# Attention scores as row-tiled quads of heads, with gelu in large blocks: one core, 2048 tokens, 32 heads of 20

## Chip, cores, metric

One core of one Trainium2 chip. The metric is device time in microseconds (us). Most executions of a kernel agree within 0.3%; some are slower. Engines: PE (TensorE), PEld (its weight loads), ACT (ScalarE), DVE (VectorE), POOL (GpSimd), SP (SyncE). "Clock" is the share of full PE clock that was granted. Three ways of placing a matmul on PE occur: column-tiled (`tile_position=(0, 32 * c)`, 32 columns each, four side by side), row-tiled (`tile_position=(32 * i, 0)`, 32 rows each) and untiled (all of PE). Going from one to another is called a change of tiling mode.

## The reference, cut

```python
qkv = xn @ wqkv                          # xn = layernorm(x), 2048 x 640, bf16
p   = softmax(q @ k.T * 20**-0.5)        # 32 heads, head size 20, 2048 x 2048 scores each
s   = (p @ v) @ wo
h   = gelu(layernorm(xn) @ w1)           # four groups of columns, shifted by 1, -1, 2, -2 tokens
x1  = xn + shifted(h) @ w2
g   = silu(x1 + gelu(layernorm(x1) @ w3) @ w4)     # w3: 640 x 1536
out = x + s * g
```

The large term is the softmax: 32 x 2048 x 2048 exponentials, on 128 lanes 1024 instructions of 1024 elements each.

## The kernel before

A planner in the kernel takes tasks with an engine, an estimated duration and the data that they read and write, and fixes each engine's order before launch. Engines then run their lists strictly in that order. MLP matmuls have the lowest priority on PE: they go where the planner believes PE to be idle.

```python
# per query block, per quad of heads: queries of head i masked over 128 rows (6 heads share a stack of rows)
T("pool", c_pool(512), lambda e, ...: e.tensor_scalar(QTP[:, qb, i, :], QT[:, st, q0:q0 + 512],
      self.maskh[:, j:j + 1], 0.0, op0=ALU.mult, op1=ALU.add), ...)
# scores of one head: four 32-column tiles, side by side
for c in range(4):
    ins = e.matmul(pb[32*c:32*c+32, 0:512], KT[:, st, kt*128 + 32*c : kt*128 + 32*c + 32],
                   QTP[:, qb, i, :], start=True, stop=True, tile_position=(0, 32 * c))
# one exp over two heads' scores, in two banks; two such pairs of banks alternate
T("act", c_act(1024), lambda e, ...: e.activation(PT[:, slot, :], self.psum[:, 1024*sb:1024*sb+1024], AF.Exp, ...))
# P*V of four heads: four 22-column tiles;  every other matmul of the kernel is column-tiled too
# gelu: evacuate, x*x, a*x+b, *x on DVE; tanh of 512 elements on ACT; (th+1)*x on DVE: 68 times
```

## Time and profile before

| | before |
|---|---|
| runs | 1073.52 and 1543.01 us, median 1308.26 |
| span of the profiled run | 1071.9 us, mean clock 0.994 |
| first exp / last exp ends / end | 47.1 / 1061.0 / 1071.9 us |
| exps, waits before them | 1024, 17.7 us |

The exps alone fill some 950 us of ACT. The lines are in the prediction below.

### The profile page before, as it was taken

The page shows a single profiled execution, that of the slowest core. Times are in us where ns is not written, and L with a number is a line of the kernel's source. Part 1 is how long each engine was busy: PE and PEld are TensorE (multiplying, and loading weights), DVE is VectorE, ACT ScalarE, POOL GpSimd, SP SyncE. Part 2 cuts the span into 40 slices and gives each one's busy share as a digit, 9 for nine tenths or more (in the row PEclk, how much of TensorE's full clock was granted, in tenths as well). Part 3 has the DMA queues.
Part 4 walks back from the last instruction along what each step waited for, and adds up shares of the span by engine and source line. Part 5 has one row for each costly group of instructions (what it writes and reads, how often), then busy time and mean ns, then how long its engine had stood idle before and what let it go on. Part 6 is the DMA issues. An engine that isn't in the chain of part 4 may idle for free.

```text
span 1071.9 us, 38329 instructions
## 1 busy us (share of the span) xinstructions
PE 937.1 (87%) x17672; PEld 395.9 (37%) x17672; DVE 547.6 (51%) x1272; ACT 1024.4 (96%) x1175; POOL 126.2 (12%) x198
## 2 busy tenths in 40 slices
PE   3899999998978899998999899889999987777786
PEld 2454454432423344443454244224443441111132
DVE  8767766792236577378647557433457310000024
ACT  7588999999989999999999999999999999999995
POOL 4202111121001110111110111110111100011100
PEclk9999999999999999999999999999999999999998
DMA  6000000020001010031111101110011000000000
GB/s 178 16 7 14 14 3 14 7 57 2 3 14 26 22 26 21 2 100 46 27 39 46 32 21 51 33 26 15 15 27 46 27 2 2 1 2 2 1 8 32
DMA packets 62968, 27.52 MB, mean 26 GB/s; under 512 B 53208, under 2 KB 62808, under 8 KB 62808
## 3 DMA queue, kind: packets, MB, share of 16 engines
q1 hardware_dynamic: 62808, 25.08, 9.1%
q8 instruction: 138, 2.26, 0.9%
q14 instruction: 22, 0.18, 0.1%
HBM read 22.45 MB, written 2.62 MB: 23 GB/s over the span
## 4 chain that ended last, share of the span: by engine, by line
ACT 63%; PE 25%; DVE 10%; issue 1%; DMA 0%; SPq 0%; DVEq 0%
ACT arena L1190 59%; PE psum L1184 11%; PE psum L1042 4%; ACT arena L1307 3%; PE psum L1198 3%; PE psum L1407 2%; PE psum L977 1%; DVE arena L1390 1%; PE psum L1470 1%; PE psum L1364 1%; DVE arena L1131 1%; ACT arena L1483 1%; DVE arena L1092 1%; PE psum L1081 1%; DVE arena L1075 1%; DVE arena L802 1%
## 5 line engine op out<-in xcount | busy, mean ns | idle before, releaser
L1190 ACT ACTIVATE arena<-psum 128x1024 bf16<-128x1024 f32 x1024 | 961.4, 1058 | 17.7 <-PE psum L1184 15.8
L1184 PE MATMUL psum<-arena 128*32 128x512 bf16 x8192 | 626.7, 382 | 83.0 <-ACT arena L1190 66.1
L1184 PEld LDWEIGHTS psum<-arena 128*32 128x32 bf16 x8192 | 157.9, 95 | 376.4 <-ACT arena L1190 327.1
L1198 PE MATMUL psum<-arena 128*22 128x512 bf16 x2048 | 199.1, 379 | 0.9 <-ACT arena L1190 0.9
L1167 POOL TENSOR_SCALAR arena<-arena 128x512 bf16<-128x512 bf16 x128 | 95.9, 763 | 677.4 <-PE psum L1184 674.2
L1206 DVE STREAM_TRANSPOSE arena<-psum 128x512 f32<-128x512 f32 x32 | 22.8, 712 | 193.9 <-PE psum L1198 193.8
L1301 DVE CAST arena<-psum 128x512 bf16<-128x512 f32 x68 | 46.8, 688 | 85.8 <-PE psum L1450 47.3
L1450 PE MATMUL psum<-arena 128*32 128x512 bf16 x960 | 79.7, 380 | 7.6 <-DVE arena L1459 7.4
L1042 PE MATMUL psum<-arena 128*32 128x512 bf16 x960 | 74.8, 385 | 2.2 <-ACT arena L895 1.0
L1470 PE MATMUL psum<-arena 128*32 128x320 bf16 x1536 | 74.6, 299 | 1.5 <-DVE arena L1459 1.5
L1198 PEld LDWEIGHTS psum<-arena 128*22 128x22 bf16 x2048 | 52.6, 93 | 57.7 <-ACT arena L1190 1.7
L1470 PEld LDWEIGHTS psum<-arena 128*32 128x32 bf16 x1536 | 40.7, 97 | 32.9 <-DVE arena L1459 3.0
L1459 DVE SCALAR_TENSOR_TENSOR arena<-arena 128x512 bf16<-128x512 bf16 x48 | 33.1, 689 | 28.2 <-ACT arena L1307 27.9
L881 PE MATMUL psum<-arena 128*32 128x128 bf16 x960 | 28.5, 242 | 19.6 <-DVE arena L823 17.8
L1307 ACT ACTIVATE arena<-arena 128x512 bf16<-128x512 bf16 x68 | 45.1, 664 | 0.0
L1236 PE MATMUL psum<-arena 128*32 128x320 bf16 x896 | 44.6, 299 | 0.1
L1364 PE MATMUL psum<-arena 128*32 128x512 bf16 x400 | 34.4, 388 | 9.6 <-DVE arena L1390 8.8
L1450 PEld LDWEIGHTS psum<-arena 128*32 128x32 bf16 x960 | 25.4, 97 | 41.7 <-DVE arena L1459 18.4
L1480 DVE SCALAR_TENSOR_TENSOR arena<-psum,arena 128x320 bf16<-128x320 f32 x32 | 14.7, 486 | 48.2 <-PE psum L1470 45.7
L1246 DVE CAST arena<-psum 128x320 bf16<-128x320 f32 x32 | 14.7, 487 | 44.7 <-PE psum L1236 44.5
L1042 PEld LDWEIGHTS psum<-arena 128*32 128x32 bf16 x960 | 24.9, 98 | 30.0 <-DVE arena L1131 1.9
L881 PEld LDWEIGHTS psum<-arena 128*32 128x32 bf16 x960 | 20.5, 107 | 36.0 <-DVE arena L823 18.8
(104 smaller groups left out, 718.2 us busy)
## 6 DMA issues: line engine op xcount, KB each, us to landing
arena<-in_B_w_dram SPq DMA_DIRECT2D x68, 160.0 KB, 2.5
arena<-in_A_x_dram SPq DMA_DIRECT2D x8, 320.0 KB, 5.9
arena<-in_A_x_dram SPq DMA_DIRECT2D x16, 160.0 KB, 2.2
out_dram<-arena SPq DMA_DIRECT2D x16, 160.0 KB, 1.8
arena<-in_B_w_dram SPq DMA_DIRECT2D x1, 1920.0 KB, 9.3
arena<-in_A_wqkv_dram SPq DMA_DIRECT2D x10, 150.0 KB, 2.8
arena<-in_A_wqkv_dram SPq DMA_DIRECT2D x1, 800.0 KB, 9.7
arena<-in_A_wo_dram SPq DMA_DIRECT2D x4, 200.0 KB
```

Source lines behind the costliest of these rows:

```text
L881: ins = e.transpose(pb[32 * c:32 * c + 32, 128 * bi:128 * bi + 128], src_of(n)[:, kc * 128 + 32 * c: kc * 128 + 32 * c + 32], ident[:, :], ...
L1042: ins = e.matmul(pb[32 * c:32 * c + 32, 0:512], Wst[:, qk, kc, 32 * c:32 * c + 32], xnT[:, kc, c0:c1], start=(kc == 0), stop=(kc == KC - 1 ...
L1167: lambda e, qb=qb, i=i, st=st, j=j, q0=q0: e.tensor_scalar(QTP[:, qb, i, :], QT[:, st, q0:q0 + 512], self.maskh[:, j:j + 1], 0.0, op0=ALU. ...
L1184: ins = e.matmul(pb[32 * c:32 * c + 32, 0:512], KT[:, st, kt * 128 + 32 * c: kt * 128 + 32 * c + 32], QTP[:, qb, i, :], start=True, stop=T ...
L1190: lambda e, sb=sb, slot=slot: e.activation(PT[:, slot, :], self.psum[:, 1024 * sb:1024 * sb + 1024], AF.Exp, scale=cfg.scale),
L1198: ins = e.matmul(pb[32 * i:32 * i + 22, 0:512], VA[:, kt, h, 0:22], PT[:, slots[i // 2], 512 * (i % 2):512 * (i % 2) + 512], start=(kt == ...
L1236: ins = e.matmul(pb[32 * c:32 * c + 32, 0:HALF], OT[:, quad, 128 * nl + 32 * c:128 * nl + 32 * c + 32], Wo[:, quad, hh * HALF:(hh + 1) * H ...
L1301: T("dve", c_dve(512, "psum"), lambda e, h=h: e.tensor_copy(xb, self.wbank(h)[:, 0:512]), reads=[wa], writes=[an(0)], name=f"{tag}_x", rel=h)
L1307: T("act", c_act(512), lambda e: e.activation(thb, wb, AF.Tanh, scale=math.sqrt(2.0 / math.pi)), reads=[an(1)], writes=[an(2)], name=f"{ta ...
L1364: ins = e.matmul(pb[32 * c:32 * c + 32, 0:512], W1s[:, ws, kc, 32 * c:32 * c + 32], y2T[i][:, kc, :], start=(kc == 0), stop=(kc == KC - 1) ...
L1450: ins = e.matmul(pb[32 * c:32 * c + 32, 0:512], W3s[:, ws, kc, 32 * c:32 * c + 32], y3T[i][:, kc, :], start=(kc == 0), stop=(kc == KC - 1) ...
L1470: ins = e.matmul(pb[32 * c:32 * c + 32, 0:HALF], GTb[:, fc, 128 * nl + 32 * c:128 * nl + 32 * c + 32], W4[:, fc, hh * HALF:(hh + 1) * HALF ...
```

## The change

Intent: take work off PE and POOL (row-tiled scores of four heads need neither masked queries nor zero rows), replace the guard against overflow by a bound for each query, walk quad by quad so that a head's projections are made one quad ahead, and run gelu as six large ACT blocks instead of 68 small tanh with DVE work around them. Core of the diff, cuts marked:

```diff
-                                for c in range(4):
-                                    ins = e.matmul(pb[32 * c:32 * c + 32, 0:512], KT[:, st, kt * 128 + 32 * c: kt * 128 + 32 * c + 32],
-                                                   QTP[:, qb, i, :], start=True, stop=True, tile_position=(0, 32 * c))
+                    return e.matmul(out, KT[32 * i:32 * i + 21, b, 128 * kt:128 * kt + 128], QT[32 * i:32 * i + 21, b, q0:q0 + 512],
+                                    start=True, stop=True, tile_position=(32 * i, 0))
 ...
+                        T("pe", 240, fn, reads=krd + qrd, writes=[("S", 2 * sb), ("S", 2 * sb + 1)], name=f"sc{self.step}")
 ...  (order: for quad: prepare quad + 1; for query block: for key tile.  Before: for query block: for quad)
 ...  (guard: per head max|k| times |q| by one small matmul, stored by DMA in row 20 of each head's 32 rows)
-        T("act", c_act(512), lambda e: e.activation(thb, wb, AF.Tanh, scale=math.sqrt(2.0 / math.pi)), ...)
+                T("act", 2600 + c_act(KC * 1024),
+                  lambda e, c0=c0: e.activation(hx[:, :, c0:c0 + 1024], hx[:, :, c0:c0 + 1024], AF.Gelu_apprx_tanh), ...)
+        T("act", 2600 + c_act(FC * 512), lambda e: e.activation(GT[:, :, :], GT[:, :, :], AF.Gelu_apprx_tanh), ...)
```

The new code can also give key tiles to DVE, but the table that says how many holds zeros only.

## The prediction

> **What bounds the kernel now.** I read the busy shares first, then the costliest groups, then who ScalarE (ACT) waited for, then ACT and TensorE (PE) in order of time.
>
> ```profile
> span 1071.9 us, 38329 instructions
> PE 937.1 (87%) x17672; PEld 395.9 (37%) x17672; DVE 547.6 (51%) x1272; ACT 1024.4 (96%) x1175; POOL 126.2 (12%) x198
> ACT  7588999999989999999999999999999999999995
> PEclk9999999999999999999999999999999999999998
> ACT 63%; PE 25%; DVE 10%; issue 1%; DMA 0%; SPq 0%; DVEq 0%
> L1190 ACT ACTIVATE arena<-psum 128x1024 bf16<-128x1024 f32 x1024 | 961.4, 1058 | 17.7 <-PE psum L1184 15.8
> L1184 PE MATMUL psum<-arena 128*32 128x512 bf16 x8192 | 626.7, 382 | 83.0 <-ACT arena L1190 66.1
> L1198 PE MATMUL psum<-arena 128*22 128x512 bf16 x2048 | 199.1, 379 | 0.9 <-ACT arena L1190 0.9
> L1167 POOL TENSOR_SCALAR arena<-arena 128x512 bf16<-128x512 bf16 x128 | 95.9, 763 | 677.4 <-PE psum L1184 674.2
> L1307 ACT ACTIVATE arena<-arena 128x512 bf16<-128x512 bf16 x68 | 45.1, 664 | 0.0
> ```
>
> ACT bounds the span: 1024 softmax exponentials of 1024 elements per partition. They waited for PE only 17.7 us. The order of time says where:
>
> ```profile
> 46.45 0.60 ACT L1065 ACTIVATE arena<-psum 128x512 bf16<-128x512 f32 x1 [8.88 <-PE psum L1042]
> 47.10 1.02 ACT L1190 ACTIVATE arena<-psum 128x1024 bf16<-128x1024 f32 x1
> 74.95 1.02 ACT L1190 ACTIVATE arena<-psum 128x1024 bf16<-128x1024 f32 x1 [1.13 <-PE psum L1184]
> 959.52 99.69 ACT L1190 ACTIVATE arena<-psum 128x1024 bf16<-128x1024 f32 x108
> 1059.94 1.02 ACT L1190 ACTIVATE arena<-psum 128x1024 bf16<-128x1024 f32 x1 [0.72 <-PE psum L1184]
> ```
>
> So the time has three parts: 47.1 us until the first exp, 1013.9 us of ACT stream (47.1 to 1061.0), 10.9 us of tail. The waits for PE lie mostly between 70 and 92 us, where the next heads' projections crowd PE. The 108 exps give a step of (99.69 - 1.02)/107 = 0.922 us.
>
> PE is next. Its 87% overstates it, since overlapping matmuls are counted to their ends; the spacing of dense groups gives the real cost:
>
> ```profile
> 72.57 1.90 PE L1042 MATMUL psum<-arena 128*32 128x512 bf16 x32
> 48.87 0.45 PE L977 MATMUL psum<-arena 128*32 128x320 bf16 x8
> 901.10 0.61 PE L1184 MATMUL psum<-arena 128*32 128x512 bf16 x8 [0.30 <-ACT arena L1190]
> ```
>
> Four 32-column matmuls run side by side: a group of width 512 costs (1.90 - 0.39)/7 = 0.216 us (0.39 is one group alone), one of 320 costs 0.45 - 0.31 = 0.14, and I estimate 0.06 for 128. By instruction counts, before has 3188 groups of 512, 960 of 320, 240 of 128: 689 + 134 + 14 = 837 us. At full clock that fits under ACT. It does not when the clock falls: PE alone would need 1543 us at a mean clock of about 837/(1543 - 20) = 0.55. I take this as the cause of the second run quoted for before (1543.01 against 1073.52); the trace shows only the fast state (mean clock 0.994).
>
> **What the Trainium skill says.**
> 1. "ScalarE: Activation LUTs", What ACT_TABLE_LOAD costs: one element per cycle whatever the function; a switch of table set is 1283 ns of load, 2.66 us with its drain. The trace has one load, of 1.28 us, so exp and tanh share a set here; no drain is visible in it.
> 2. "TensorE: Matmul & The Clock Gate", Part 3: matmuls in different 32-row groups run concurrently (four of K=32, N=512 ran 3.07 times as fast). The trace has column groups only, which do run together.
> 3. "TensorEngine Tiling (Array Packing)", Key Properties: "Changing tiling mode (not just tile) drains the TensorE". This trace never changes mode.
> 4. The TensorE page again, Part 1: an idle window of about 3.4 us drops the PE clock to half. The trace's gaps are below that.
>
> **The change, part by part.**
>
> *Scores.* Before: each head's queries are masked on POOL (L1167, 128 x 763 ns) and multiplied over 128 rows, so an exp needs two groups, 0.43 us. After: four heads lie at row tiles of 32 and an exp needs two 21-row matmuls of 128 columns in different row groups and banks, 0.216 us if they overlap. Saved: 1024 x 0.216 = 221 us of PE and all 96 us of POOL, both off the path. The exps are unchanged: 1024, none given to VectorE (the table that would do so holds zeros).
>
> *Projections.* Padding to 32 costs PE 320 groups instead of 240 (+17 us); the squared-norm matmuls go (-10 us). PE after: 837 - 221 + 17 - 10 = about 624 us, plus drains. At least two mode changes per exp; a drain exposes about 0.39 - 0.216 = 0.17 us, so 2 x 1024 x 0.17 = 350 us, total about 970. Still under ACT's 1014, but thin in the stages with MLP matmuls.
>
> *VectorE.* The five-instruction gelu chain (688 + 437 + 309 + 456 + about 690 ns, 68 times) becomes one evacuation: -68 x 1.9 = -129 us. Other per-head guard work shrinks too. All hidden before: no gain in time, only fewer late releases.
>
> *ACT stream, before.* In the stretch 640 to 700 us a tanh takes a slot of 0.52 and a silu tanh 0.62 us: 68 x 0.52 + 16 x 0.62 = 45.3. With 1.5 for late query copies and 16.7 of waits, the exps have 1013.9 - 63.5 = 950, 0.927 each.
>
> *ACT stream, after.* Exps 950. Gelu on whole blocks: two of 5120 and four of 6144 elements at 0.833 ns (0.427 us per 512) plus about 0.15: 2 x 4.4 + 4 x 5.3 = 30. Silu: eight of 1280, 8 x 1.16 = 9. Gelu needs another table set: each of six goes there and back, 12 loads. At 1.28 us: 15; at 2.66: 32. I take 1.6: 19. Sum 1008, against 997 before without waits. Thus the batching saves 45 - 39 = 6 us and pays back 15 to 32 in table loads: a net loss of about 12.
>
> *Waits in the stream.* Most of the 16.7 us came from projections crowding PE, now spread over quads and with scores half as dear. I keep 8.
>
> *Start.* The last LayerNorm write on ACT is at 20.2 us before and after. Then transposes, evacuated alternately by ACT and VectorE without the accumulator reads (0.2 us each on 12), done at about 27; last K and Q tiles 2 x 5 x 0.216 + 0.7 = 3, at 30. The new bound is a serial chain: max over 2048 (a 512 max takes 0.68; 2.3), mask 0.2, matmul 0.39, evacuation 0.69, a DMA into the spare row (about 2.2, as small loads land), score 0.39, with waits 7: 37 us. The quad's weights now come as 40-byte rows in eight DMAs; I add 5 for them and for ordering: 42 against 47.1.
>
> *Tail.* Same chain of transpose, reciprocal, scale, transpose, last output matmuls, store: 11.
>
> Sum: 42 + 1008 + 8 + 11 = 1069 us. Against the fast run (1073.5) that is the same; the large PE saving buys almost nothing there, since PE did not bound it.
>
> In the slow state it buys much: 624/0.55 = 1135 us of PE work plus some 45 of start and tail, about 1180 against 1543.
>
> **The rivals.**
> - *PE becomes the bound through mode drains.* For: the skill's sentence; 0.17 us is more than half a score group. If weight loads (0.095 us) are exposed too, a switch costs 0.27 and two exps in an MLP stage need 0.43 + 0.22 + 0.9 + 4 x 0.27 = 2.6 against 1.85 of ACT. Three of eight quads at up to 1.4 times: up to 140 us more, 1200. Against: the scheduler has freedom to cluster the other matmuls, and most stages have few.
> - *Large gelus starve PE.* An ACT block of 5.3 us plus two loads leaves PE without score banks for about 7 us, enough to drop the clock; six times. Restarting at half clock still gives about 0.86 + 0.43 us per two exps, below 1.85, so perhaps 1 us each: 1075.
> - *The stream closes up more than I think.* Table loads at 1.28, no waits, first exp at 37: 37 + 1004 + 2 + 11 = 1054. This is the floor of the fast state; it is 1.8% below 1073.5.
> - *A late input in a fixed order.* Each engine runs a fixed list; one late gelu input stalls all exps behind it. For: the planner does not model drains. It would add 10 to 40 us.
>
> **Range and chances.** Fast to fast I expect 1069, mostly 1050 to 1100: same 0.65, faster 0.17, slower 0.18. But the time on record for before is 1308, the middle of one fast and one slow run; against that even a mixed pair after, (1069 + 1180)/2 = 1125, is faster by 14%. I do not know which comparison decides; I weigh the median at two thirds: faster 0.67, same 0.25, slower 0.08. The range, 1042 to 1150, holds the fast state and a mixed pair.
>
> **What would show it.** ACT busy about 1025 us again, 13 table loads, exps about 0.93 apart; first exp at 37 to 47; PE busy well below 937 with scores near half of 626.7; POOL under 4%. I am wrong if exps wait for PE by more than 30 us (drains), if a gelu waits for VectorE or PE, if a table load takes far from 1.3 us, or if the first exp comes after 50. A slow run of the changed kernel near 1180 would confirm the clock account of 1543; no slow run at all would leave it open.

## The result

| | before | after |
|---|---|---|
| runs, us | 1073.52, 1543.01 | 1199.82, 1210.49 |
| median, us | 1308.26 | 1205.15 |
| mean clock of the profiled run | 0.994 | 0.751 |

Fast to fast the changed kernel is slower: ratio 1.1227, 95% interval 1.1014 to 1.1441. A ratio here is the mean span of one kernel's fast runs over that of the other's of the same rounds, so it is not quite the ratio of the medians that are quoted. Against the median of 1308 the changed kernel looks 8% faster, but that median is the middle of a fast and a slow run, and no run of the kernel before took 1308 us.

The page of the changed kernel, the lines that answer to those of before (L1087 is the exp, L1071 the scores, L1096 P*V, L687 the helper through which nearly all other matmuls go; out of each group: busy us, mean ns, then idle time before it and what ended it):

```profile
span 1197.9 us, 25310 instructions
PE 1059.6 (88%) x11568; PEld 315.3 (26%) x11568; DVE 330.1 (28%) x655; ACT 1065.3 (89%) x1095; POOL 27.8 (2%) x52
ACT  7689999989889988999888898799998999988886
PEclk9989998789555556555799898898955555578766
PE 52%; ACT 40%; DVE 4%; DMA 3%; issue 1%; ACTq 0%; SPq 0%; POOL 0%; DVEq 0%
L1087 ACT ACTIVATE arena<-psum 128x1024 bf16<-128x1024 f32 x1024 | 987.4, 1026 | 107.1 <-PE psum L1071 93.1
L1071 PE MATMUL psum<-arena 21*128 21x512 bf16 x2048 | 506.5, 491 | 79.0 <-ACT arena L1087 63.9
L1096 PE MATMUL psum<-arena 128*22 128x512 bf16 x2048 | 256.4, 491 | 0.7 <-ACT arena L1087 0.7
```

PE executes a third fewer instructions (11568 for 17672) and is still the larger part of the chain, 52% instead of 25%. The exps wait 107 us instead of 18. And the clock row, flat at 9 before, has two troughs at half.

ACT in order of time (start, length, what, how many merged, in brackets the idle time before and its releaser):

```profile
42.19 5.83 ACT L1087 ACTIVATE arena<-psum 128x1024 bf16<-128x1024 f32 x6 [5.80 <-PE psum L1071]
468.46 27.88 ACT L1087 ACTIVATE arena<-psum 128x1024 bf16<-128x1024 f32 x30 [0.57 <-PE psum L1071]
497.56 1.02 ACT L1087 ACTIVATE arena<-psum 128x1024 bf16<-128x1024 f32 x1 [1.23 <-PE psum L1071]
611.52 3.08 ACT L1087 ACTIVATE arena<-psum 128x1024 bf16<-128x1024 f32 x3 [0.27 <-PE psum L1071]
653.15 3.02 ACT L1087 ACTIVATE arena<-psum 128x1024 bf16<-128x1024 f32 x3 [0.27 <-PE psum L1071]
656.19 1.28 ACT L1370 ACT_TABLE_LOAD   x1
657.49 5.32 ACT L1370 ACTIVATE arena<-arena 128x6144 bf16<-128x6144 bf16 x1
662.83 1.28 ACT L1087 ACT_TABLE_LOAD   x1
```

Start and table loads are as expected. The exps now run in strings with waits of up to 1.2 us between them. A wait costs twice: an exp takes 1.023 us by itself but a step in a string takes about 0.917 (median 0.916 before, 0.920 after), so each exp after a wait also loses 0.106 us of overlap.

Where the 126 us came from, by the exps' own records (profiled runs, us):

| | before | after | difference |
|---|---|---|---|
| until the first exp | 47.1 | 42.2 | -4.9 |
| waits before exps | 17.7 (38 of over 0.03 us) | 101.3 (362 of over 0.03 us) | +83.6 |
| lost overlap, 0.106 for each wait | 4.0 | 38.4 | +34.4 |
| rest of the ACT stream (exps, gelu, silu, loads) | 992 | 1005 | +13 |
| tail | 11.0 | 11.2 | +0.2 |

(The 101.3 counts from the first exp on; the page's 107.1 has the 5.8 before the first one too.) So 118 of the 126 us are exps that wait for scores. What makes PE late, with PE's own work cut? This stretch of PE, in an MLP stage at full clock, shows it:

```profile
691.02 0.39 PE L1071 MATMUL psum<-arena 21*128 21x512 bf16 x2
691.34 0.40 PE L1096 MATMUL psum<-arena 128*22 128x512 bf16 x4
691.56 0.60 PE L687 MATMUL psum<-arena 128*32 128x512 bf16 x8
692.10 0.39 PE L1071 MATMUL psum<-arena 21*128 21x512 bf16 x2
692.41 0.81 PE L687 MATMUL psum<-arena 128*32 128x512 bf16 x16
693.15 0.39 PE L1071 MATMUL psum<-arena 21*128 21x512 bf16 x2
693.47 0.40 PE L1096 MATMUL psum<-arena 128*22 128x512 bf16 x4
693.70 0.71 PE L687 MATMUL psum<-arena 128*32 128x320 bf16 x16
694.34 0.39 PE L1071 MATMUL psum<-arena 21*128 21x512 bf16 x2
694.66 0.86 PE L687 MATMUL psum<-arena 128*32 128x320 bf16 x20
695.46 0.39 PE L1071 MATMUL psum<-arena 21*128 21x512 bf16 x2
```

From a score pair to P*V it is 0.32 us start to start, from P*V to another column-tiled group 0.22. Over the whole trace at full clock the medians are 318 ns from scores to P*V and 222 ns from P*V to others, and the dense spacing of the same 512 columns is 216: entering or leaving the row tiles costs 0.10 us, the cost that the prediction calls a drain. (After a 320-wide group the medians are 242 ns to the next scores and 136 to another group.) At half clock it is 537 against 427, 0.11 us. The pair itself costs no more than one matmul, so its two row tiles do run together.

The weight loads show what a change takes away. The first line is from the stretch above; the second is a P*V group of run e1 below, which changes no mode:

```profile
691.34 0.10 PEld L1096 LDWEIGHTS psum<-arena 128*22 128x22 bf16 x4 [0.23 <-issue]
1000.64 0.10 PEld L1113 LDWEIGHTS psum<-arena 128*22 128x22 bf16 x4
```

Without a change the first weights are loaded 0.22 us before their matmul (at 1000.86), under the group before; after a change they come at 691.34, as late as the matmul itself. Behind a 512-wide group at full clock the medians are 214 ns ahead in e1, and 2 to 4 ns at a change. The 0.10 us is the whole cost of a change; how much of it is emptying PE and how much the load that is no longer hidden, no run separates.

In the stretch of PE, four exps' worth of PE takes 695.46 - 691.02 = 4.44 us, 1.11 each, with eight changes of 0.10. Without them it would be 0.91, just under the exp's step of 0.922: the planner, which knows nothing of the drains, had filled PE to the brim.

Two theories, then. **D**: the changes of tiling mode cost 0.10 us each and make PE late. **C**: with fewer matmuls PE falls to half clock and is late for that reason. Rivals: the new order, the preparation of each quad, or the gelu blocks.

### The profile page after: what moved, and what is told of

Same layout as the page of the kernel before. It is cut to its first block, busy times and chain, and to the rows that moved or that the text cites. A ratio compares the mean times of both kernels' runs of the same rounds, so it can differ in the third digit from the quotient of the medians.

```text
span 1197.9 us, 25310 instructions
## 1 busy us (share of the span) xinstructions
PE 1059.6 (88%) x11568; PEld 315.3 (26%) x11568; DVE 330.1 (28%) x655; ACT 1065.3 (89%) x1095; POOL 27.8 (2%) x52
## 4 chain that ended last, share of the span: by engine, by line
PE 52%; ACT 40%; DVE 4%; DMA 3%; issue 1%; ACTq 0%; SPq 0%; POOL 0%; DVEq 0%
ACT arena L1087 36%; PE psum L687 27%; PE psum L1071 15%; PE psum L1096 8%; DMA arena<-in_B_w_dram 3%; ACT arena L1370 2%; DVE arena L845 1%; PE psum L908 1%; ACT L1087 1%; ACT arena L1383 1%; PE psum L944 0%; DMA arena<-in_A_x_dram 0%; ACT L1370 0%; DVE arena L1158 0%; DVE arena L1166 0%
## 5 line engine op out<-in xcount | busy, mean ns | idle before, releaser
L1087 ACT ACTIVATE arena<-psum 128x1024 bf16<-128x1024 f32 x1024 | 987.4, 1026 | 107.1 <-PE psum L1071 93.1
L1071 PE MATMUL psum<-arena 21*128 21x512 bf16 x2048 | 506.5, 491 | 79.0 <-ACT arena L1087 63.9
L687 PE MATMUL psum<-arena 128*32 128x320 bf16 (+1 forms) x6480 | 409.3, 370 | 36.9 <-ACT arena L1370 20.8
L1096 PE MATMUL psum<-arena 128*22 128x512 bf16 x2048 | 256.4, 491 | 0.7 <-ACT arena L1087 0.7
L1071 PEld LDWEIGHTS psum<-arena 21*128 21x128 bf16 x2048 | 100.9, 95 | 493.7 <-ACT arena L1087 358.4
L687 PEld LDWEIGHTS psum<-arena 128*32 128x32 bf16 x6480 | 159.5, 102 | 184.1 <-issue 72.6
L1096 PEld LDWEIGHTS psum<-arena 128*22 128x22 bf16 x2048 | 51.2, 90 | 168.7 <-issue 160.2
L987 DVE TENSOR_SCALAR arena<-psum,arena 128x512 bf16<-128x512 f32 x32 | 23.7, 750 | 112.8 <-PE psum L687 111.0
L1379 DVE TENSOR_TENSOR arena<-psum,arena 128x320 bf16<-128x320 f32 x32 | 14.3, 485 | 111.1 <-PE psum L687 111.1
L1327 DVE TENSOR_TENSOR arena<-psum,arena 128x320 bf16<-128x320 f32 x32 | 14.4, 486 | 39.8 <-PE psum L687 39.6
L1168 DVE STREAM_TRANSPOSE arena<-arena 128x512 bf16<-128x512 bf16 x32 | 23.8, 744 | 0.7
L1166 DVE TENSOR_TENSOR arena<-arena 128x512 bf16<-128x512 f32 x32 | 22.0, 687 | 0.7
```

Of the source, the lines that this page charges most:

```text
L687: ins = e.matmul(pb[32 * c:32 * c + 32, 0:N], lhsT(k, c), rhs(k, c), start=(k == 0), stop=(k == nk - 1), tile_position=(0, 32 * c))
L987: T("dve", c_dve(512), lambda e, h=h, c0=c0: e.tensor_scalar(KT[:, b, c0:c0 + 512], self.wbank(h)[:, 0:512], self.eaug[:, 0:1], None, op0= ...
L1071: return e.matmul(out, KT[32 * i:32 * i + 21, b, 128 * kt:128 * kt + 128], QT[32 * i:32 * i + 21, b, q0:q0 + 512], start=True, stop=True, ...
L1087: lambda e, sb=sb, slot=slot: e.activation(PT[:, slot, :], self.psum[:, 1024 * sb:1024 * sb + 1024], AF.Exp, scale=cfg.scale),
L1096: ins = e.matmul(pb[32 * i:32 * i + 22, 0:512], VA[:, ql, kt, i, :], PT[:, slots[i // 2], 512 * (i % 2):512 * (i % 2) + 512], start=first, ...
L1166: return e.tensor_tensor(OnT[:, ob, :].rearrange("p (a b) -> p a b", b=32), in0, in1, op=ALU.mult)
```

## The experiments

All ran on the chip; times are medians, and the edits are shown shortened. Kernels of one job shared the runs of the kernel before, whose medians were 1072.01, 1072.42 and 1071.29 us. Except where said, the outputs were correct.

**e1: the old score form in the new kernel.** Masks are built on POOL as before.

```diff
-    return e.matmul(out, KT[32*i:32*i+21, b, 128*kt:128*kt+128], QT[32*i:32*i+21, b, q0:q0+512], ..., tile_position=(32*i, 0))
+    for c in range(4):
+        ins = e.matmul(out[32*c:32*c+32, :], KT[:, b, 128*kt+32*c:128*kt+32*c+32], QTP[:, qb, i, :], ..., tile_position=(0, 32*c))
-    T("pe", 240, fn, ...)
+    T("pe", 440, fn, ...)
```

> The changed kernel with its scores alone put back to the old form: four 32-column matmuls over all 128 rows per head, with queries masked on POOL; quad order, guard, gelu and all else stay. Theory D+C (drains at the change between row tiles and column tiles, 0.10 us each in the trace, plus a PE clock that drops to half because the PE has too little to do): no mode change is left and PE activity is back to about 0.54 us per 0.92 us, so mean clock above 0.97, exps waiting for PE under 30 us, time 1055 to 1085. Rival O (the new order, the per-quad preparation or the gelu blocks are to blame): the scores do not matter, waits stay near 100 us, time above 1150.

1080.44 us, ratio to before 1.0085 (1.0047 to 1.0124), clock 0.986, waits before exps 13.0 us. As D and C expected; rival O falls. The row-tiled scores cost nearly the whole loss, some 125 us; all other parts of the change together cost 8 us. (The plan's cost of a pair goes from 240 to 440 ns here as well; that is about what the matmuls of a pair take in each form, 0.22 and 0.43 us.)

**e2: useless P*V work to hold the clock up** in the quads without much MLP work.

```diff
+    NREP = 3 if quad in (2, 3, 6, 7) else 1
+    for r in range(NREP):
         for i in range(4): ins = e.matmul(pb[32*i:32*i+22, 0:512], VA[...], PT[...],
-                       start=first, stop=final, ...)
+                       start=first and r == 0, stop=final and r == NREP - 1, ...)
```

> The changed kernel with each P*V group done three times in quads 2, 3, 6 and 7 (numerator and denominator grow alike, so the result stays right): useless PE work of 0.43 us per two exps, column tiles, no further mode change, same order. Theory C (half clock from too little PE activity): half-clock time falls from 599 us to below 250, idle before exps at half clock from 57 us to below 20, time 1120 to 1155 although the PE does more. Theory D alone (drains, the clock harmless): clock may rise but time stays within 15 us of the changed kernel or grows.

1194.65 us; clock 0.91 to 0.92 in the three fast runs, so the filling does hold the clock up, and the time hardly moves (1205 for the changed kernel). This speaks against theory C alone, though the filling is itself work for PE; e5 and e7 settle it. The profiled run was a slower one (1208.73), so its figures are only a hint: waits at half clock fell from 56.7 to 48.5 us only, not below 20 as C expected; at half clock for 7% of the time instead of 92% and 75%, quads 2 and 3 took 125 and 141 us for 134 and 144; quad 7 took 144 for 140.

**e3: dearer scores in the plan**, instructions unchanged.

```diff
-    T("pe", 240, fn, ...)                       # score pair
+    T("pe", 440, fn, ...)
-    T("pe", c_pe(4, 512), fnpv, ...)
+    T("pe", c_pe(4, 512) + 100, fnpv, ...)
```

> The changed kernel with the planner told that a score pair costs 440 ns instead of 240 and a P*V group 319 instead of 219; the instructions are the same, only their fixed order differs. Theory D with over-packing (the planner fills every idle PE slot of the MLP stages by a cost without drains): idle before exps at full clock falls from 45 us to below 20, MLP matmuls spread over more of the span, time 1130 to 1165. If the plan is not at fault: within 2% of the changed kernel.

1330.73 us, ratio 1.2394: a miss, and in the other direction. At full clock the waits do vanish (9.6 us before 326 exps), but the evenly spread work leaves PE at half clock for 979 us, where exps wait 216 us. The new order also has more changes of mode, 1784 for 1528:

```profile
300.00:440.00 140.00, 136.89 (x1108) 29.31 (x1108) 43.40 (x96) 113.47 (x116) 5.21 (x9) 0.58 0.14 33
720.00:860.00 140.00, 136.09 (x1102) 30.07 (x1104) 28.60 (x45) 101.85 (x102) 0.00 (x0) 0.56 0.08 14
```

(Stretches of e3; columns: us, busy time of PE, PEld, DVE, ACT, POOL, clock, DMA share, GB/s.) PE is busy for 137 of 140 us, by the profile's count, and still granted half clock. So the half clock seems harmless only where little needs doing.

**e4: tanh in place of gelu in the changed kernel** (wrong).

```diff
-    AF.Gelu_apprx_tanh
+    AF.Tanh
```

> The changed kernel with tanh in place of gelu in the six large blocks (wrong result on purpose; same elements, but tanh shares the table set of exp): takes away the 12 table loads and nothing else. Theory G (the batching's table loads cost what the prediction said): 12 x 1.28 to 1.6 = 15 to 19 us less, time about 1182 to 1190. If PE is what the exps wait for after each block anyway: less than 8 us gained.

1198.75 us, some 6 us below the changed kernel's 1205.15 and within the scatter of their runs. Where exps wait for PE, table loads are not what sets the time.

**e5: mode changes without row tiles and with full PE activity.** As e1, but untiled.

```diff
-    for c in range(4): ins = e.matmul(out[32*c:32*c+32, :], KT[:, b, 128*kt+32*c:128*kt+32*c+32], QTP[:, qb, i, :], ..., tile_position=(0, 32*c))
+    return e.matmul(out, KT[:, b, 128*kt:128*kt+128], QTP[:, qb, i, :], start=True, stop=True)
```

> As e1 (masked queries over 128 rows, two matmuls of 512 streaming steps' worth per exp, the same plan costs), but each head's scores are one untiled 128-column matmul instead of four 32-column ones: the PE streams exactly as much as in e1, no row tiles, but the tiling mode changes around the scores as in the changed kernel. Theory D (any change of mode costs 0.10 us): start spacing of a score pair and the group after it rises from 0.43 to 0.53 us, some 1500 to 1800 changes are 150 to 185 us of PE, time 1110 to 1190. If only row tiles cost: 1075 to 1090, as e1.

1193.68 us, ratio 1.1147, clock 0.983; 4 us above the range that D gave. The first fence is e1, the second e5, PE in order of time, both at full clock:

```profile
1000.42 0.60 PE L1087 MATMUL psum<-arena 128*32 128x512 bf16 x8
1000.86 0.39 PE L1113 MATMUL psum<-arena 128*22 128x512 bf16 x4
```

```profile
1099.90 0.60 PE L1086 MATMUL psum<-arena 128*128 128x512 bf16 x2
1100.43 0.40 PE L1110 MATMUL psum<-arena 128*22 128x512 bf16 x4
```

The pair of heads takes 0.44 us to the next group in e1 and 0.53 in e5, as D expected. e5 has about 1670 changes, and with them 75.9 us of waits at full clock in 570 pieces. Same streaming, same plan costs, same clock as e1, 113 us more.

**e6: low PE activity without mode changes** (wrong: one head of two is computed, the exp reads its bank twice).

```diff
-    for jj in range(2):
+    for jj in range(1):                                # plan cost 240
         ins = score(e, self.bank(2 * sb + jj)[:, :], 2 * a + jj)
-    e.activation(PT[:, slot, :], self.psum[:, 1024*sb:1024*sb+1024], AF.Exp, ...)
+    e.activation(PT[:, slot, :] as 2 x 512, bank(2 * sb) read twice, AF.Exp, ...)
```

> As e1 (32-column tiles, no mode change) but only one of the two heads of a pair is computed and the exp reads that bank twice (wrong result on purpose; ACT work is the same): PE activity is as low as in the changed kernel, without row tiles and without drains; score cost in the plan 240. Theory C (the clock follows how much the PE streams): half-clock time above 300 us, as with row tiles. Rival R (the clock monitor does not see 21-row tiles as work): half-clock time below 60 us. In both cases, if drains and not the clock cost the time, time 1065 to 1100; if the half clock alone is harmful, above 1130.

1078.33 us, ratio 1.0048, clock 0.864. Half-clock time is 294 us, at the edge of what C expected and far from rival R's 60: column-tiled matmuls that leave PE with as little streaming as the changed kernel let the clock fall too, for half as long (599 us there). But the half clock costs next to nothing here, as exps at half clock wait 8.5 us.

**e7: mode changes injected into e1.**

```diff
+    e.matmul(self.bank(2*sb)[:, 0:32], KT[32*i:32*i+21, b, 128*kt:128*kt+128], QT[32*i:32*i+21, b, q0:q0+32],
+             start=True, stop=True, tile_position=(32 * i, 0))        # overwritten at once
     for jj in range(2): ins = score(...)
```

> e1 plus one tiny row-tiled matmul (21 rows, 128 columns, only 32 wide, overwritten at once by the real scores) before every score pair: two mode changes per exp with hardly any streaming, same plan, PE activity not lower than in e1. Theory D: 2 x 0.10 us per exp, 1024 times, about 205 us of PE plus 25 of streaming on top of e1's 845: PE about 1075 us and the bound in every MLP stage, time 1150 to 1260 with the clock near 1.0. If drains are hidden behind the waits for ACT: within 2% of e1's 1080.

1220.34 us, ratio 1.1377, clock 0.985, exactly 2048 changes. PE's useful work is that of e1; a 32-wide matmul before each pair costs 140 us. The tiny matmul takes 114 ns until the first real one starts. Theory D is shown by adding its cost, with nothing but 1024 matmuls of 32 columns beside it.

**e8: e3 with every P*V group done twice.**

```diff
     # as e3, and the loop of e2 with
+    NREP = 2
```

> e3 (the plan with dearer scores, which got slower, 1331 us, with 979 us of its span at half clock) with every P*V group done twice, same order of tasks: more PE work. If e3 lost its time to the half clock: half-clock time falls below 300 us and time below 1220. If e3's order itself is bad (late inputs, drains): no better than 1310.

1301.81 us (1272.28 to 1341.87): inconclusive. Only the run of 1272.28 is fast, and it lies between the two forecasts. The filling held the clock up in part only (643.5 us at half clock, in a slower run's profile). There, quads 0 to 2, at half clock for 0 to 28%, took 131, 138 and 128 us; quads 3, 6 and 7, at 85 to 87%, took 164 to 183. That goes with the half clock as e3's cause, but quads 4 and 5, at 33 and 46%, took 161 and 163, and the forecast was not met.

**e9: the plan with one true drain per pair.**

```diff
-    T("pe", 240, fn, ...)                       # score pair
+    T("pe", 340, fn, ...)
```

> The changed kernel with the planner's cost of a score pair at 340 ns, which is 240 plus the one drain of 0.10 us that the trace shows before it, P*V left at 219. If the plan only lacked the drains: MLP stages stop being over-packed and time falls to 1120 to 1170. If spreading the MLP matmuls lets the clock fall instead, as in e3 (cost 440: 979 us at half clock): half-clock time above 700 us and time above 1200.

1197.96 us in the fast run and 1219.55 in the slow one: no gain, neither forecast right. In the profile, which is of the slower run, waits at full clock fell from 44.7 to 23.8 us and waits at half clock rose from 56.7 to 99.2. It looks as if work moved out of the MLP stages lands where the clock is low.

**e10: e1 with tanh for gelu** (wrong).

```diff
     # as e1, and
-    AF.Gelu_apprx_tanh
+    AF.Tanh
```

> e1 (1080 us, bound by ACT) with tanh in place of gelu in the six large blocks (wrong result on purpose): takes 12 table loads off an engine that is the bound. Predicted term: 12 x 1.28 to 1.6, so 15 to 19 us less, 1061 to 1065; [...]in the changed kernel itself the same edit (e4) gave only 6 us, so if table loads are free anyway: above 1074.

1074.17 us, 6.3 us less than e1: just inside the forecast for free loads (above 1074), though they were not quite free. 12 x 1.28 = 15.4 us of loads left ACT, but in the profiles, one run each, the waits before exps rose from 13.0 to 19.9 us. It seems that nearly half of what the loads took had been covering work of PE, and came back as waits.

**e11: a version meant to beat both**: e1 with gelu as tanh of a DVE polynomial, tanh still in six large blocks.

```diff
-    e.activation(GT[:, :, :], GT[:, :, :], AF.Gelu_apprx_tanh)
+    # DVE per 512:  w = x*x;  w = 0.044715*w + 1;  w = w*x
+    e.activation(GW, GW, AF.Tanh, scale=math.sqrt(2.0 / math.pi))     # block of 5120 or 6144
+    # DVE per 512:  x = (w + 1) * x;  the factor 0.5 goes into the next evacuation
```

> A correct version meant to beat both: e1 with gelu as tanh of a polynomial made on VectorE (as in the kernel before), but tanh still in the same six large blocks, so no table set is changed. ACT bound: e1 less 15 to 19 us, 1060 to 1068, that is 0.4 to 1.1% under the kernel before (1072). If VectorE's 130 us of added work delays the blocks' inputs and ACT waits at them: 1075 or more.

1070.61 us, ratio to before 0.9996 (0.9977 to 1.0014), the same as before and 11% less than the changed kernel. It misses both forecasts (1060 to 1068, and 1075 or more) and does not beat the kernel before. One table load is left:

```profile
L1104 ACT ACTIVATE arena<-psum 128x1024 bf16<-128x1024 f32 x1024 | 953.9, 1048 | 28.5 <-PE psum L1087 27.4
L1303 ACT ACTIVATE arena<-arena 128x6144 bf16<-128x6144 bf16 (+1 forms) x6 | 30.4, 5066 | 0.0
L885 ACT ACT_TABLE_LOAD x1 | 1.3, 1283 | 0.8 <-PEq L1450 0.8
```

**e12: low activity with mode changes**: e6 with the untiled matmul of e5 (wrong).

```diff
-    for c in range(4): ins = e.matmul(out[32*c:32*c+32, :], ..., tile_position=(0, 32*c))      # as in e6, one head of two
+    return e.matmul(out, KT[:, b, 128*kt:128*kt+128], QTP[:, qb, i, :], start=True, stop=True)
```

> e6 (one head of each pair computed, read twice, wrong on purpose) with the scores as one untiled 128-column matmul: PE activity as in e6 and in the changed kernel, mode changes as in the changed kernel, no row tiles. e6 had 45 and 63% of quads 2 and 6 at half clock, the changed kernel 92 and 97%. If the drains make the clock fall (they are idle time for it): above 85% here. If it is the row tiles: 45 to 65%. Time, by the drains: 1120 to 1200, against 1078 for e6.

1153.97 us, ratio 1.0769, clock 0.826, 402 us at half clock. Time as D expected. On the clock neither forecast fits: quad 2 was at half clock for 61%, quad 6 for 95%.

The five kernels that answer the main question:

| | no mode change | mode changes (untiled scores) | mode changes (row tiles) |
|---|---|---|---|
| two matmul times per exp | e1 1080 us, clock 0.986 | e5 1194, 0.983 | |
| one matmul time per exp | e6 1078, 0.864 | e12 1154, 0.826 | changed kernel 1205, 0.751 |

Down a column the activity changes (and the plan's cost of a pair, 440 above and 240 below), along a row the mode changes. Activity alone is worth 2 us without them. Mode changes alone are worth 113 us at high and 76 us at low activity.

## Why the prediction was wrong, point by point

- **What bounds before; ACT stream.** Right. ACT is the bound of every variant without mode changes. The stream after, less its waits and lost overlap, is 1005 us; 1008 was predicted.
- **Start and tail.** Right in size: first exp at 42.2 (42 predicted), tail 11.2 (11). The start was partly luck: 5 of the 42 were an allowance for weights and ordering that was not worked out.
- **Waits in the stream: "I keep 8".** This step failed. It measured 101 us, with 34 more of lost overlap than before, a cost that the sum had no term for. The prediction's own sign, "exps wait for PE by more than 30 us (drains)", came true. 8 came from the argument that PE had room, and that most of the 17.7 us before lay where projections crowd PE, "between 70 and 92 us". That reading was wrong too: 7.4 us lay there, and 10.0 came after 169 us.
- **The room on PE.** The mechanism was named and its size guessed too high, and yet it was dismissed. The prediction had 2 x 1024 changes of 0.17 us, 350 us; the runs show 1528 of 0.10, about 156 us, so PE's work is some 780 us at full clock, further below ACT's 1014 than I had it. A total below the bound proved nothing: the planner puts MLP work wherever it sees a gap, so in those stages the drains had no gap to go to (1.11 us per exp for 0.92). "PE becomes the bound through mode drains" stood among the rivals with up to 1200 us (close to 1205 by luck: it had 1.3 us per exp in three quads of eight, where the stretch shows 1.11), and the argument held against it, that the scheduler has freedom to cluster, was wrong: the order is fixed by a plan that does not know the drains.
- **The clock.** Predicted to stay, since the trace's gaps were short. It fell to half for 599 us in all (2 of them after the last instruction), 24 times: 17 with no PE gap above 0.53 us in the 7 us before, none with PE idle for more than 2.8 us by then. The trace of before had two such falls already, at 312 and 1063 us, in gaps of 1.8 and 2.6 us; they were overlooked. e6 shows that low activity is enough for that, and e5 and e7 that drains cost as much without the fall. In e3 the obvious cure, to spread the MLP work, failed with PE at half clock; e8 could not show that this was the reason.
- **Gelu blocks.** 13 loads of 1.283 us, as predicted, and back at once (656.19 + 1.28 = 657.47; gelu starts at 657.49). The 2.66 us that the prediction quoted for a switch of set does not show here: all 12 switches take 1.31 us from the end of the instruction before to the start of the one after (here 656.17 to 657.49), and the measurement decides. The stream's net effect of about +12 is matched by the +13 in the table above. Where ACT is the bound, taking the loads away gains 6 us (e10), not 15 to 32.
- **The slow run of before.** I took 1543 us for a run at about 0.55 of the clock. The clock of that run is not on record, but one of the runs of the kernel before beside e1 took 1834.02 us with a granted clock of 1.0, so a run can be slower still at full clock. The account is left without support; what slows such a run is open. None of the 42 runs of the changed kernel and its variants shows anything like it.
- **Range and chances.** 1205 lies outside 1042 to 1150. The median of before with its slow half took two thirds of the weight, and the fast comparison got only 0.18 for slower.

Left open: the changed kernel is 51 us above e12 though both stream alike and change modes about as often (1528 and, counted by the weight loads, 1526 times). It has 200 us more of half clock, and quads with equal shares of half clock take equal time (quad 0: 144 and 143 us; quad 6: 121 and 120). The traces say where the time goes: waits at full clock, with their lost overlap, take 74 us in the changed kernel and 80 in e12, at half clock 65 and 13. So the whole difference lies at half clock, and nearly half of the changed kernel's waiting does. That points to the clock as an addition to the drains, but no run raised the clock of the row-tiled kernel without adding PE work. Why row tiles get less clock than untiled matmuls of the same length is open too.

## What to carry to other kernels

Before tiling one kind of matmul differently from its neighbours, count the changes of tiling mode that the order will contain and put their cost into each stage's budget, not into the total: PE had 230 us to spare over the span and none where it mattered. Work saved on PE where it is not the bound can lower PE's clock (0.994 to 0.751 here), so keep measuring the granted clock with the busy time.

## What the Trainium skill lacked or had wrong

- "TensorEngine Tiling (Array Packing)", Key Properties, says that a change of tiling mode drains TensorE and gives no figure. Here a change costs 0.10 us at full clock (318 against 216 ns start to start) and 0.11 at half (537 against 427), in both directions, and also between untiled 128-column and 32-column matmuls (309 against 216). e7 pays 140 us for 2048 of them.
- "TensorE: Matmul & The Clock Gate", Part 1, lets the clock fall after an idle window of about 3.4 us; its passage on a second failure mode adds that frequent short idles between groups of matmuls make the clock swing, without a length or a share. Here it fell without a gap of that size: in e6, with about 0.32 us of score and P*V matmuls per exp of 0.92 us, 24 of 32 falls had no PE gap above 0.52 us in the 7 us before; and in e3 PE stayed near half clock while it was counted busy for 136 of 140 us. What share of activity keeps the clock up, and how row tiles count, no page says.
